# Opening of a fused mLSTM and MoE kernel: v of the first two tiles ahead of q and k on SyncE's queue

## The chip, the cores and the metric

The kernel runs on one core of a Trainium2 chip, in one launch. A core has TensorE (PE), VectorE (DVE), ScalarE (ACT), GpSimd (POOL) and SyncE (SP). PE multiplies matrices, and PEld is its weight load, which overlaps the multiplication. SP and ACT each have a queue of DMA transfers; their issues are listed as SPq and ACTq. A DMA is issued by an instruction of about half a microsecond on its engine and lands some microseconds later. The metric is device time in microseconds (us), as a median of runs; smaller is better.

## What is computed

An mLSTM attention with gates over 2 batches of 8 heads, 768 positions and head size 40, whose output of 1536 x 320 goes through a mixture of four experts and then through a gated MLP:

```python
m_new = np.maximum(f_gate[:, :, t] + m, i_gate[:, :, t])
f_stab = np.exp(f_gate[:, :, t] + m - m_new)
i_stab = np.exp(i_gate[:, :, t] - m_new)
C = f_stab * C + i_stab * np.einsum('bhd,bhe->bhde', vt, kt)
n = f_stab * n + i_stab * kt
y[:, :, t] = o * np.einsum('bhde,bhe->bhd', C, qt) / np.maximum(abs(n . qt), 1.0)
...
out += p[:, e:e + 1] * (np.maximum(x @ w1[e], 0.0) @ w2[e])     # 4 experts, 320 -> 1024 -> 320
...
return (((x @ w_a) * (x @ w_b)) @ w_out)                       # 320 -> 1536 -> 320
```

## The kernel before

**Tiles.** The attention goes by twelve tiles n = 0 to 11, each 128 positions of one batch with its eight heads; tiles 0 and 1 are the first 128 positions of batch 0 and of batch 1. Heads 0 to 3 and 4 to 7 of a tile are its halves hh = 0 and hh = 1. Within a tile the recurrence is worked out as a masked 128 x 128 product of q and k, weighted by exponentials of the gates, times v.

**Loads of a tile.** `load_qk(n, hh)` (L329, its DMA at L341) brings q and k of one half, transposed: of the first four tiles 48 rows of 4096 B, to partitions 0 to 47 for hh = 0 and to partitions 64 to 111 for hh = 1 of one tile `qk_t`. `load_kvo(n)` (L369) reserves the tile `kvo_t` and loads k, v and the carried q in rows; for tiles 0 and 1 it only reserves. Their v comes by `load_v(n)` (L673, DMA at L674): 128 rows of 1476 B. Their k in rows comes much later by `load_k`. `load_gates(j)` (L378) loads gates of position block j into `gt` (DMA at L382 for block 0, on ACT's queue, and L384 for later ones, on SP's). `load_rsel` loads a small selection matrix. The generators `w0`, `w1`, `w2` load the first expert blocks' weights in eight pieces each (L93) and split each piece into a high part `wh` (L78) and a low part `wl` (L102).

**The order.** The first part is not scheduled by a planner. A list `ev` holds (key, function, arguments), is sorted by key, and its functions are called in that order; keys below 0 come before the first expert product. Each function appends its instructions to the engines it uses, and each engine runs its own in that order. So the list's order is the order of each queue. A DMA also takes one of eight semaphores (DMAHW0 to DMAHW7) in turn, and the ninth issue on waits until the earlier DMA with the same semaphore has landed.

**Work of the opening.** In PE's order: eight warm-up products (`warm_up`, L648), four mask products (`mask_of`, L485), the products of q and k of tile 0 (`scores2(0)`, L518, which take the halves by turns), the gate products of tile 0 (`weights_of`, L495), `scores2(1)`, `weights_of` of tile 1, and then the products with v of both tiles (`s2a`, L541), `scores2(2)`, the transposition into x (`s3a`, L154 to L156), and the first expert products (`Item.a`, L210). Beside it DVE works out the gates (`gate1`, L393, on), builds the right operand of `weights_of` (`build_R`, L479, and L477 on ACT), multiplies scores and weights (`s1b`, L530), scales and gates the result (`s2x`, L570 to L580) and writes the low part of x (`split_lo`, L145 and L147). ACT takes the exponentials (`w_exp`, L500). After x of tiles 0 and 1 stands, DVE's next instruction is `gate1(1)`, which needs gates of block 1, and after it comes the eviction `hl` of the first expert product (L278), for whose PSUM buffer the third expert product waits.

Of the kernel before, what the change touches and what calls it, by code (L numbers as in the profile page):

```python
# [13 lines left out]
AF = mybir.ActivationFunctionType  # L14
# [37 lines left out]
def mlstm_moe_kernel(ctx, tc, gates, qk, qc, kvo, dp, w1b, w2b, ident_d, bdmask_d, rsel_d, exp_d, out):  # L52
    nc = tc.nc
# [26 lines left out]
    def piece1(i, s, pool, lo_eng, apart=False, dma=None, hi_eng=nc.scalar):  # L80


        if s == 0:
            wblk[i] = (pool.tile([P, WB1], F32R, tag="wh", name=f"wh{i}"), pool.tile([P, WB1], F32R, tag="wl", name=f"wl{i}"))
        wh, wl = wblk[i]
        st = WB1 // NP1
        cs = slice(s * st, (s + 1) * st)
        at = LAND[i][s] if i < 3 else None
        if at is not None:
            raw = sums[:, at * st:(at + 1) * st]  # L90
        else:
            raw = rawp.tile([P, st], F32, tag="raw", name=f"raw{i}_{s}")
        (dma or nc.sync).dma_start(raw, w1b[i][:, cs])  # L93
        yield
        if apart:
            yield
        copy_on(hi_eng, wh[:, cs], raw)
        yield
        parts = 2 if i < 3 and lo_eng is nc.gpsimd else 1
        for k in range(parts):  # L100
            ps = slice(s * st + k * st // parts, s * st + (k + 1) * st // parts)
            lo_eng.tensor_tensor(wl[:, ps], raw[:, k * st // parts:(k + 1) * st // parts], wh[:, ps].bitcast(F32), op=ALU.subtract)  # L102
# [206 lines left out]
    with ExitStack() as c1:  # L309
# [353 lines left out]
        w0, w1, w2 = ([piece1(i, f, wp0, nc.vector if LOENG[i][f] == "v" else nc.gpsimd, hi_eng=nc.gpsimd if i == 0 and f < 2 else nc.scalar) for f in range(NP1)] for i in range(3))  # L663
# [41 lines left out]
        def x_lo(n):  # L705
# [3 lines left out]
        P_ = nc.gpsimd  # L709
        A_ = nc.scalar  # L710
        ev = [
            (-40, load_gates, 0, A_), (-39.9, load_rsel, nc.sync), (-39.8, load_qk, 0, 0, A_), (-39.7, load_qk, 0, 1, nc.sync),
            (-39.6, load_qk, 1, 0, A_), (-39.5, load_qk, 1, 1, nc.sync), (-39.4, load_kvo, 1), (-39.3, load_kvo, 0), (-39.2, table, AF.Exp),
            (-39.1, load_v, 0), (-39, load_v, 1), (-38.9, go, w0[0:1]), (-38.8, fill_R, 0), (-38.7, ones, ), (-38.6, go, w0[3:4]),
            (-38.5, warm_up, WARM, pw), (-38.4, go, w0[1:2]), (-38.3, go, w0[2:3]), (-38.2, fill_R, 1), (-38.1, load_qk, 2, 1),
            (-38, load_o, 0, nc.sync), (-37.9, load_qk, 2, 0), (-37.8, go, w0[4:5]), (-37.7, go, w0[5:6]), (-37.6, go, w0[6:7]),
            (-37.5, load_ident, ), (-37.4, load_o, 1, nc.sync), (-37.3, go, w0[7:8]), (-37.2, go, w1[0:1]), (-37.1, load_gates, 1),
# [359 lines left out]
```

## Time and profile before

| | |
|---|---|
| median of 3 runs | 598.3 us (597.3, 598.3, 599.43) |
| the profiled execution | 597.87 us |
| its span in the trace | 596.1 us |
| PE busy | 586.3 us (98%) |
| DVE, ACT, POOL busy | 395.2, 268.2, 190.5 us |
| granted clock of PE | 1.0 in all stretches of the page |

The page gives for each engine the time in which it had an instruction running. A busy PE is not PE at its peak. The chain of waits is followed back from the last instruction to what released each step, the timeline lists instructions in order, and a table by stretches gives busy time, the granted clock and what the DMA engines moved. The idle time ahead of an instruction and what ended it stand in brackets.

### The profile page before, as it was taken

What the parts mean: (1) busy time and instruction counts of PE and PEld (TensorE: products, weight loads), DVE (VectorE), ACT (ScalarE), POOL (GpSimd) and SP (SyncE); (2) the same over time, 40 slices, a digit from 0 to 9 for tenths busy, and PEclk for the clock granted to TensorE, in tenths of its full rate; (3) what the DMA queues carried; (4) which work ended last, traced back from release to release, by engine and by line L of the source; (5) the groups of instructions that cost most, each with busy time, mean ns of one, the idle gap of its engine ahead of it and who ended that gap; (6) DMA issues with size and microseconds to landing.
All of it is one profiled execution on the core that took longest, in us unless ns stands there. A gap on an engine that the chain in (4) does not pass through costs nothing.

```text
span 596.1 us, 14965 instructions
## 1 busy us (share of the span) xinstructions
PE 586.3 (98%) x6108; PEld 555.6 (93%) x6108; DVE 395.2 (66%) x813; ACT 268.2 (45%) x606; POOL 190.5 (32%) x246
## 2 busy tenths in 40 slices
PE   8999999999999999999999999999999999999997
PEld 5798999999899999999999999999898989898887
DVE  6888877876423665645466666688688787875444
ACT  7879478683232444433233332334455534341211
POOL 3966665650010333544022231221323222311000
PEclk9999999999999999999999999999999999999999
DMA  8979648750211333332111211515312121200012
GB/s 238 272 227 241 177 135 231 186 154 1 60 40 54 80 86 107 92 89 52 36 40 38 57 40 39 143 53 153 115 42 73 39 58 52 63 21 2 1 38 97
DMA packets 34626, 55.48 MB, mean 93 GB/s; under 512 B 3861, under 2 KB 22461, under 8 KB 34557
## 3 DMA queue, kind: packets, MB, share of 16 engines
q10 hardware_dynamic: 18992, 27.07, 16.4%
q1 hardware_dynamic: 14893, 25.48, 15.9%
q0 software_dynamic: 672, 1.97, 1.2%
q8 instruction: 48, 0.79, 0.6%
q14 instruction: 21, 0.17, 0.1%
HBM read 50.15 MB, written 3.96 MB: 91 GB/s over the span
## 4 chain that ended last, share of the span: by engine, by line
PE 81%; DVE 7%; DMA 6%; ACT 2%; ACTq 2%; issue 2%; SPq 0%; DVEq 0%
PE psa L230 28%; PE psy L255 26%; PE psb L230 8%; PE psa L210 6%; DMA gt<-in_gates 3%; PE pt_y L541 2%; PE psy L289 2%; PE psy L291 2%; PE psy L290 2%; DMA qk_t<-in_qk 2%; PE pt_i L547 1%; PE pt_c L526 1%; PE pt_u L604 1%; DVE acc L300 1%; DVE g L914 1%
## 5 line engine op out<-in xcount | busy, mean ns | idle before, releaser
L255 PE MATMUL psy<-wh,hh 64*128 64x320 f32 x848 | 179.0, 306 | 1.5 <-ACT acc L890 1.5
L255 PE MATMUL psy<-wl,hh 64*128 64x320 f32 x848 | 178.7, 306 | 0.0
L255 PE MATMUL psy<-wh,hl 64*128 64x320 f32 x848 | 178.7, 306 | 0.0
L230 PE MATMUL psa<-xh,wh 64*128 64x512 f32 x648 | 147.5, 388 | 0.2 <-DVE g L914 0.2
L255 PEld LDWEIGHTS psy<-wh,hh 64*128 64x128 f32 x848 | 131.5, 184 | 2.6 <-ACT acc L890 1.9
L255 PEld LDWEIGHTS psy<-wh,hl 64*128 64x128 f32 x848 | 131.6, 184 | 0.0
L255 PEld LDWEIGHTS psy<-wl,hh 64*128 64x128 f32 x848 | 131.4, 184 | 0.0
L230 PE MATMUL psa<-xh,wl 64*128 64x512 f32 x468 | 109.4, 387 | 0.0
L230 PEld LDWEIGHTS psa<-xh,wh 64*128 64x128 f32 x648 | 92.9, 184 | 3.9 <-DVE g L914 0.8
L230 PE MATMUL psa<-xl,wh 64*128 64x512 f32 x432 | 95.3, 387 | 0.0
L911 DVE SCALAR_TENSOR_TENSOR hl<-psa,hh 128x512 fp32r<-128x512 f32 x72 | 46.3, 685 | 72.4 <-ACT hh L910 72.4
L134 POOL TENSOR_TENSOR wl<-tp,lf 128x272 fp32r<-128x272 f32 x48 | 39.1, 814 | 122.3 <-DVE tp L133 111.4
L230 PEld LDWEIGHTS psa<-xh,wl 64*128 64x128 f32 x468 | 69.6, 184 | 2.7
L230 PE MATMUL psb<-xh,wh 64*128 64x512 f32 x216 | 69.7, 388 | 0.0
L131 POOL TENSOR_TENSOR lf<-lf,sq 128x272 f32<-128x272 f32 x48 | 38.1, 795 | 95.4 <-ACT wh L130 72.2
L910 ACT ACTIVATE hh<-psa 128x512 fp32r<-128x512 f32 x72 | 39.1, 596 | 64.1 <-PE psy L255 33.4
L230 PEld LDWEIGHTS psa<-xl,wh 64*128 64x128 f32 x432 | 62.9, 184 | 2.5
L230 PE MATMUL psb<-xh,wl 64*128 64x512 f32 x180 | 58.2, 387 | 0.0
L130 ACT CAST wh<-tp 128x272 fp32r<-128x272 f32 x48 | 20.2, 420 | 68.7 <-DVE tp L127 66.4
L102 POOL TENSOR_TENSOR wl<-raw,wh 128x352 fp32r<-128x352 f32 (+1 forms) x30 | 28.4, 950 | 70.0 <-ACT wh L78 70.0
L230 PE MATMUL psb<-xl,wh 64*128 64x512 f32 x144 | 44.2, 387 | 0.0
L914 DVE TENSOR_TENSOR g<-psa,bs 128x512 f32<-128x512 f32 x36 | 24.7, 685 | 28.1 <-ACT bs L913 27.9
(147 smaller groups left out, 1254.5 us busy)
## 6 DMA issues: line engine op xcount, KB each, us to landing
raw<-in_w2b ACTq DMA_DIRECT2D x48, 272.0 KB, 2.8
qk_t<-in_qk SPq DMA_DIRECT2D x16, 480.0 KB, 6.2
raw<-in_w1b ACTq DMA_DIRECT2D x40, 176.0 KB, 2.3
acc<-in_w1b SPq DMA_DIRECT2D x22, 176.0 KB, 4.8
kvo_t<-in_kvo SPq DMA_DIRECT2D x10, 364.5 KB, 6.2
og_t<-in_kvo SPq DMA_DIRECT2D x6, 320.0 KB, 4.9
dz_t<-z_t ACTq DMA_DIRECT2D x12, 160.0 KB, 2.7
qc_t<-in_qc SPq DMA_DIRECT2D x10, 180.0 KB, 4.3
```

Of the source, the lines that this page charges most:

```text
L102: lo_eng.tensor_tensor(wl[:, ps], raw[:, k * st // parts:(k + 1) * st // parts], wh[:, ps].bitcast(F32), op=ALU.subtract)
L130: nc.scalar.copy(wh[:, cs], tf)
L131: nc.gpsimd.tensor_tensor(lf, lf, sq, op=ALU.mult)
L134: nc.gpsimd.tensor_tensor(wl[:, cs], tf, lf, op=ALU.add)
L210: nc.tensor.matmul(ps, l, r, start=(i == 0), stop=(i == len(prs) - 1))
L230: return nc.tensor.matmul(ps[g], w[rows, o:o + P], x, start=start, stop=stop)
L255: ms = [nc.tensor.matmul(ps[t], l[rows, t * P:(t + 1) * P], w[rows, off:off + DM], start=start, stop=stop) for t, rows in zip(two, (UP, DN))]
L289: nc.tensor.matmul(ps, lh, wh[:, off:off + DM], start=(fi == 0), stop=False)
L290: nc.tensor.matmul(ps, lh, wl[:, off:off + DM], start=False, stop=False)
L910: nc.scalar.activation(hh, ps[f], AF.Relu)
L911: nc.vector.scalar_tensor_tensor(hl, ps[f], 0.0, hh.bitcast(F32), op0=ALU.max, op1=ALU.subtract)
L914: nc.vector.tensor_tensor(g, ps[2 * f + 1], bs, op=ALU.mult)
```

## The change

Nine entries of the list get other keys. `load_kvo(1)`, `load_kvo(0)`, `load_v(0)` and `load_v(1)` come directly behind `load_rsel`, ahead of the four `load_qk` of tiles 0 and 1; the table load for the exponential follows them and keeps its place among ACT's work. No function is changed and no instruction added or removed.

```diff
-            (-40, load_gates, 0, A_), (-39.9, load_rsel, nc.sync), (-39.8, load_qk, 0, 0, A_), (-39.7, load_qk, 0, 1, nc.sync),
-            (-39.6, load_qk, 1, 0, A_), (-39.5, load_qk, 1, 1, nc.sync), (-39.4, load_kvo, 1), (-39.3, load_kvo, 0), (-39.2, table, AF.Exp),
-            (-39.1, load_v, 0), (-39, load_v, 1), (-38.9, go, w0[0:1]), (-38.8, fill_R, 0), (-38.7, ones, ), (-38.6, go, w0[3:4]),
+            (-40, load_gates, 0, A_), (-39.9, load_rsel, nc.sync), (-39.8, load_kvo, 1), (-39.7, load_kvo, 0), (-39.6, load_v, 0),
+            (-39.5, load_v, 1), (-39.4, load_qk, 0, 0, A_), (-39.3, load_qk, 0, 1, nc.sync), (-39.2, load_qk, 1, 0, A_),
+            (-39.1, load_qk, 1, 1, nc.sync), (-39, table, AF.Exp), (-38.9, go, w0[0:1]), (-38.8, fill_R, 0), (-38.7, ones, ), (-38.6, go, w0[3:4]),
```

On SP, at the start of the program: `kvo_t` is v of tiles 0 and 1, `qk_t` the halves hh = 1 of q and k of tiles 0 and 1, and `acc` the first pieces of expert weights, which land in a buffer that later holds sums.

```order
 L680 DMA rsel<-in_rsel_d 112x17
+L674 DMA kvo_t<-in_kvo 128x369 x2
 L341 DMA qk_t<-in_qk 48x1024 x2
-L674 DMA kvo_t<-in_kvo 128x369 x2
 L93 DMA acc<-in_w1b 128x352 [waits DMAHW0_49]
 L93 DMA acc<-in_w1b 128x352 [waits DMAHW1_49]
```

The two loads of v passed the two loads of q and k on SP's queue. ACT's queue, with gates, half 0 of tile 0 and half 0 of tile 1, has the order it had.

On PE, from the last mask products to the first products with v: `pt_c` are scores, `pt_a` the gate products, `pt_y` the products with v.

```order
 L485 MATMUL pt_a<-upper,one 128x512 x3
 L518 MATMUL pt_c<-qk_t 128x128 [waits DMAHW2_49]
-L518 MATMUL pt_c<-qk_t 128x128 [waits DMAHW3_49]
+L518 MATMUL pt_c<-qk_t 128x128 [waits DMAHW6_49]
 L518 MATMUL pt_c<-qk_t 128x128 x6
 L495 MATMUL pt_a<-Rr_110,LT_108 128x512 [waits DVE_49,Activation_49]
 L495 MATMUL pt_a<-Rr_110,LT_108 128x512 [waits Activation_49]
 L518 MATMUL pt_c<-qk_t 128x128 [waits DMAHW4_49]
-L518 MATMUL pt_c<-qk_t 128x128 [waits DMAHW5_49]
+L518 MATMUL pt_c<-qk_t 128x128 [waits DMAHW7_49]
 L518 MATMUL pt_c<-qk_t 128x128 x6
 L495 MATMUL pt_a<-Rr_111,LT_108 128x512 [waits DVE_49] x2
```

PE's order stays. Half 1 of q and k of tile 0 moved from semaphore 3 to 6, that of tile 1 from 5 to 7, and v of the two tiles from 6 and 7 to 3 and 5.

## Rows read from the trace of the kernel before

**Rows 1.** The page's first part: busy time, share of the span, instructions.

```profile
PE 586.3 (98%) x6108; PEld 555.6 (93%) x6108; DVE 395.2 (66%) x813; ACT 268.2 (45%) x606; POOL 190.5 (32%) x246
```

**Rows 2.** The chain of waits, opening: start us, us, what.

```profile
2.21 5.23 DMA qk_t<-in_qk
...
13.53 5.27 DMA gt<-in_gates
...
18.83 0.81 DVE fa L393
...
20.15 0.42 DVE hl L278
```

**Rows 3.** Timeline of PE: start us, us, instruction, count [idle before].

```profile
4.42 2.01 PE L485 MATMUL pt_a<-upper,one 128*128 128x512 f32 x4
6.36 1.16 PE L518 MATMUL pt_c<-qk_t 40*128 40x128 f32 x16
8.00 0.69 PE L495 MATMUL pt_a<-Rr,LT 112*128 112x512 f32 x2 [0.48 <-DVE Rr L479]
8.62 1.16 PE L518 MATMUL pt_c<-qk_t 40*128 40x128 f32 x16
9.72 0.73 PE L495 MATMUL pt_a<-Rr,LT 112*128 112x512 f32 x2
10.38 2.64 PE L541 MATMUL pt_y<-kvo_t,w_t 128*64 128x82 f32 x64
...
20.63 0.39 PE L210 MATMUL psa<-xh,wh 128*128 128x256 f32 x1 [1.05 <-DVE hl L278]
...
24.70 0.39 PE L210 MATMUL psa<-xh,wh 128*128 128x256 f32 x1
```

**Rows 4.** Timelines of ACTq and SPq: issues of the opening.

```profile
1.57 1.08 ACTq L341 DMA_DIRECT2D qk_t<-in_qk  x2
...
1.26 1.00 SPq L341 DMA_DIRECT2D qk_t<-in_qk  x2
2.30 0.90 SPq L674 DMA_DIRECT2D kvo_t<-in_kvo  x2
```

**Rows 5.** Issues of ACTq, single: bytes, us from issue to landing.

```profile
gt<-in_gates ACTq DMA_DIRECT2D x1, 112.0 KB, 3.4
...
qk_t<-in_qk ACTq DMA_DIRECT2D x1, 192.0 KB, 4.6
```

**Rows 6.** Issues of SPq, single, same columns.

```profile
qk_t<-in_qk SPq DMA_DIRECT2D x1, 192.0 KB, 3.8
rsel<-in_rsel_d SPq DMA_DIRECT2D x1, 7.4 KB, 1.7
...
kvo_t<-in_kvo SPq DMA_DIRECT2D x1, 184.5 KB, 5.6
```

**Rows 7.** Busy time by stretches; last columns: granted clock, DMA share, GB/s.

```profile
2.00:7.00 5.00, 5.00 (x21) 2.73 (x21) 2.43 (x8) 3.69 (x5) 0.34 (x2) 1.00 0.91 216
7.00:8.00 1.00, 0.52 (x10) 0.36 (x7) 0.97 (x3) 1.00 (x4) 0.00 (x0) 1.00 1.03 336
8.00:9.00 1.00, 1.00 (x8) 0.68 (x10) 1.00 (x2) 0.56 (x2) 0.00 (x1) 1.00 1.07 393
10.00:11.00 1.00, 1.00 (x18) 0.64 (x19) 0.54 (x2) 0.74 (x2) 1.00 (x3) 1.00 0.99 180
12.00:13.00 1.00, 1.00 (x28) 0.85 (x24) 0.90 (x5) 0.99 (x3) 0.23 (x1) 1.00 0.98 166
```

**Rows 8.** Timeline of DVE and POOL around the first expert products.

```profile
17.73 0.29 DVE L147 TENSOR_TENSOR xh<-pt_x,xh 64x128 fp32r<-64x128 f32 x1
18.83 0.80 DVE L393 TENSOR_TENSOR_SCAN fa<-gt,fa 112x128 f32<-112x128 f32 x1 [0.80 <-DMA gt<-in_gates]
...
15.98 0.24 POOL L78 COPY x_t<-x_t 128x64 f32<-128x64 f32 x1 [0.48 <-DVE x_t L580]
16.17 7.86 POOL L102 TENSOR_TENSOR wl<-acc,wh 128x176 fp32r<-128x176 f32 x14
```

## The prediction

> **What bounds the kernel.** I read the page's first part, then the chain of waits, then the timelines of the first 25 us, then the table by stretches. PE is busy for 586.3 of 596.1 us [rows 1]: a gain or loss must come from the few places where PE stands idle, and the change touches only the opening. In the chain [rows 2] the reader is to see that the opening is a row of transfers, q and k of tile 1 (landed at 7.44), then the gates of block 1 (issued at 13.53, landed at 18.80), then DVE's `fa` and `hl`, which let PE go on. PE's timeline [rows 3] says where PE stood: 0.48 us before the gate products at 8.00, waiting for DVE, and 1.05 us before the third expert product at 20.63, waiting for `hl`. From 20.63 to 25 us it works nearly without gaps, so what the opening adds there is carried on.
>
> **What moves.** Nothing is added or removed. Two loads of v (184.5 KB each) pass two of q and k (192 KB each) on SP's queue [rows 6]. Half 1 of tile 0 was first there, issued at 1.26 [rows 4] and landed after 3.8 us, at 5.1 [rows 6]. Half 0 comes on ACT's queue, issued at 1.57 [rows 4], landed after 4.6 us, at 6.2 [rows 5], and the scores began at 6.36 [rows 3], so half 0 came last and half 1 had 1.3 us to spare. The loads of v landed at about 8.35 (second issue near 2.75, plus 5.6) [rows 4, 6] and were first wanted at 10.38 [rows 3]: v had two microseconds to spare and gains nothing by landing earlier. So the change takes time from the load with 1.3 us of cover and gives it to one with 2.
>
> **When half 1 of tile 0 lands now.** Ahead of its end stand the selection matrix (7.4 KB), the gates (112), two loads of v (369) and itself (192), and, since ACT's queue runs beside SP's and the sizes are alike, also both halves on ACT's queue (384): 1064 KB or 1.09 MB [rows 5, 6]. From 2 to 7 us the queues moved 216 GB/s [rows 7], 1.08 MB by 7.0; the rest is there at 7.03. Landing comes after that. In the old order all of the eight first loads are 1256 KB or 1.287 MB, which at 216 and then 336 GB/s [rows 7] are through at 7.6, and the last landed at 8.35: 0.75 us later. So half 1 lands at 7.8. Low end: the second load on ACT's queue is not ahead of it, 0.89 MB, through at 6.15, landed at 6.9. High end: it takes the place in time of the last load before, 8.35. I take 7.8, for the two queues shared the engines evenly before too: the third load on ACT's queue landed at 7.44 [rows 2], after both of SP's.
>
> **What that moves on PE.** The scores of tile 0 take 1.16 us [rows 3]: 7.8 to 8.96. The gate products behind them on PE stood at 8.00 because of DVE, not because of the scores, which were over at 7.52; that 0.48 us is used up first. They start at 9.0, 1.0 us later (0.1 at the low end, 1.5 at the high). Queued behind the waiting scores on PE are the gate products, the scores of tile 1 and the products with v, and ACT's exponentials and DVE's multiplications wait for these, so all attention work of tiles 0 and 1 goes 1.0 us later. The scores of tile 1 need half 1 of tile 1, the next load on SP's queue: at 173 GB/s (mean of 180 and 166, the two stretches with one such load in flight [rows 7]) it lands 1.14 us after 7.8, at 8.95, and PE comes to these scores 0.62 us after 9.0: 0.65 us of cover.
>
> **What hides it later.** DVE had written x at 18.02 and stood 0.80 us until the gates of block 1 landed [rows 8]. Delayed by 1.0 it is done at 19.02; of the delay 0.8 falls into that idle time. What then counts is when those gates land. The same bytes are ahead of them, but in other company. Before, q and k of both halves went at the same time on two queues, inside the stretch at 216 GB/s; now v runs beside half 0, and the two loads of half 1 come last, mostly alone of their kind, which ran at 173. Two loads are 393 kB: 2.27 us at 173 instead of 1.82 at 216, 0.45 us later. Bounds: all four loads at 173, 0.9 later; or the mixing of v with half 0 gains up to 0.8 (more than 0.80 cannot count, as DVE's idle time is no longer). I take 0.45, since both rates are this kernel's own. The gates land at 19.25, `fa` begins at 19.28, which is behind 19.02, `hl` goes with it, and the third expert product goes from 20.63 to 21.1.
>
> A rule that speaks against the change: the Trainium skill, "SBUF — State Buffer", section "Door 1: The DMA port swizzle", says that partitions 0 to 63 reach only eight of the sixteen ports by which DMA writes and partitions 64 to 127 the other eight. Loads of half 0 and half 1 side by side would then use all ports, and half 1 alone half of them. The trace agrees in kind: 180 and 166 GB/s with one load of 48 rows in flight against 393 with loads of 128 rows [rows 7]. By the page's 27.2 GB/s a port, eight ports give 218 GB/s (an estimate), the two loads would take 1.80 us, the 0.45 would go, and the time would be that of the first rival.
>
> **Other work.** POOL began its long run of low parts behind its copy of x at 15.98 and ended fourteen pieces at 24.03 [rows 8]; the fifth expert product, which takes the last of them, began at 24.70 [rows 3]. Begun 1.0 us later it ends at 25.0, against a product that itself goes to 25.15: 0.15 us of cover are left. The load of weights behind these loads lands some tenths later; POOL and ACT wait for x or for the exponentials there. The gates of block 0 are first on ACT's queue as before; were they earlier, the scores would still be waited for.
>
> **Sum.** Profiled execution 597.87 (span 596.1): +0.45, 598.3. The median of the runs is 0.43 above the profiled one, so 598.3 becomes 598.75; I say 598.8.
>
> **Rivals.**
> - *Hidden.* Half 1 lands by 6.84 (8.00 less the scores' 1.16), PE's 0.48 us covers it, and the gates of block 1 land as before. For it: the low end, 6.9. Against it: the even sharing. Time 598.3.
> - *Faster.* Small rows of v beside half 0 move better than q beside q; the gates of block 1 land up to 0.8 us earlier, DVE's idle time before `fa` goes and the third expert product comes earlier. For it: 393 GB/s with 128-row loads alone [rows 7]. Against it: x must be done early too. 597.5.
> - *Nothing is absorbed.* Half 1 lands at 8.35, the attention is 1.5 us later, and POOL's run of low parts, not DVE, sets the expert products. It decides from about 1.15 us on, where POOL's cover (0.67 us plus the 0.45 of DVE) ends. 0.85 to 1.5 us: up to 599.8.
> - *Slower, by the clock.* PE stands idle from 6.43 (end of the masks [rows 3]) to 7.8 where it had none. The clock reads 1.00, which is 2.4 GHz, in all stretches [rows 7]; if it falls to 1.2 GHz, the gate products, the scores of tile 1 and the products with v (0.69, 1.16, 0.73 and 2.64 [rows 3], 5.2 us) double, and less the 0.8 to 1.0 us that DVE's idle time takes, some 4 us stay: 602.7. It decides from the idle time at which the clock falls. For it: the mask products ran at 0.50 us each, the gate products of the same 512 columns at 0.35, so PE was slower shortly before. Against it: after 1.05 us of idle before 20.63 the clock read nothing else.
>
> **Chances.** Forecast 0.46 (598.5 to 599.1), hidden 0.22, faster 0.08, nothing absorbed 0.15, clock 0.09. The range leaves out the clock and a tail: the faster case less 0.2 is 597.3, nothing absorbed plus 0.5 is 600.3. A measurement of this kernel can tell some 0.3%, 1.8 us, from no change: all cases but the clock lie inside, save the end of the unabsorbed one, so slower 0.15, faster 0.03, same 0.82.
>
> **What would show it.** In the trace after: half 1 of tile 0 landing near 7.8, and PE's scores at L518 waiting for it from 6.43 (right), or starting by 6.84 (hidden); the first gate product at 9.0; v landed long before its first use; DVE's idle time before the second `fa` near 0.25 and gates of block 1 landing near 19.25; third expert product at 21.1. Wrong it is if the third expert product starts before 20.5 or after 22, if the granted clock drops, or if PE's gaps after 25 us change.

## The result, and the profile after

The changed kernel takes 602.82 us (median of 602.55, 602.74, 602.89 and 603.7) beside 598.05 for the kernel before (four runs too); the ratio is 1.008, 95% interval 1.0058 to 1.0101. It is slower by 4.8 us where 0.5 was forecast. The number is that of the rival that was given 0.09, and the clock did fall; that its price came out to 0.1 us is in part luck, as told below.

The profiled execution took 602.74 us, its span 600.9. The timeline of PE answers to [rows 3]; columns as there.

```profile
4.42 1.54 PE L485 MATMUL pt_a<-upper,one 128*128 128x512 f32 x4
5.89 0.49 PE L518 MATMUL pt_c<-qk_t 40*128 40x128 f32 x2
8.75 2.07 PE L518 MATMUL pt_c<-qk_t 40*128 40x128 f32 x14 [2.38 <-DMA qk_t<-in_qk]
10.75 1.22 PE L495 MATMUL pt_a<-Rr,LT 112*128 112x512 f32 x2
11.90 2.08 PE L518 MATMUL pt_c<-qk_t 40*128 40x128 f32 x16
13.91 1.22 PE L495 MATMUL pt_a<-Rr,LT 112*128 112x512 f32 x2
15.06 4.18 PE L541 MATMUL pt_y<-kvo_t,w_t 128*64 128x82 f32 x64
...
24.71 0.39 PE L210 MATMUL psa<-xh,wh 128*128 128x256 f32 x1
```

PE began the scores of tile 0 at 5.89, with half 0 landed, and stood idle for 2.38 us at the first product that needs half 1. What comes then is not only later but slower: the gate products take 1.22 us instead of 0.69, the scores of tile 1 2.08 instead of 1.16, the products with v 4.18 instead of 2.64. The third expert product starts at 24.71, 4.08 us later.

By stretches (last columns granted clock, DMA share, GB/s), which answers to [rows 7]:

```profile
2.00:7.00 5.00, 4.37 (x13) 2.05 (x11) 2.68 (x9) 3.97 (x6) 0.34 (x2) 1.00 0.94 220
7.00:8.00 1.00, 0.00 (x0) 0.00 (x0) 1.00 (x2) 0.79 (x3) 0.00 (x0) 1.00 1.06 159
8.00:9.00 1.00, 0.25 (x2) 0.25 (x4) 0.79 (x2) 0.00 (x0) 0.00 (x0) 0.69 0.98 150
9.00:15.00 6.00, 6.00 (x34) 4.31 (x34) 1.29 (x2) 1.34 (x3) 3.05 (x6) 0.50 1.06 286
15.00:18.00 3.00, 3.00 (x45) 2.94 (x46) 1.65 (x5) 2.97 (x6) 0.00 (x0) 0.50 1.10 359
18.00:19.00 1.00, 1.00 (x24) 1.00 (x22) 0.86 (x3) 1.00 (x3) 0.19 (x1) 0.69 1.09 323
19.00:25.00 6.00, 5.90 (x51) 4.48 (x49) 5.06 (x16) 4.16 (x13) 5.14 (x10) 1.00 0.92 278
```

The granted clock is 1.00, which is 2.4 GHz, until within the microsecond from 8 to 9 us, then 0.50, which is 1.2 GHz, and 1.00 again from within 18 to 19 us: some ten microseconds at the low level, begun while PE stood idle. PE is 100% busy from 9 to 18 us, and this is the stretch in which it loses most. In the kernel before no stretch of the opening shows less than 1.00. For the first microseconds of a run this column does not tell the level, though: the second experiment shows why, and how the products' own times tell it.

The loads, issues and then single issues with the time to landing, answer to [rows 4] and [rows 6]:

```profile
1.27 1.01 SPq L674 DMA_DIRECT2D kvo_t<-in_kvo  x2
2.32 0.89 SPq L341 DMA_DIRECT2D qk_t<-in_qk  x2
```

```profile
kvo_t<-in_kvo SPq DMA_DIRECT2D x1, 184.5 KB, 3.5
...
qk_t<-in_qk SPq DMA_DIRECT2D x1, 192.0 KB, 6.4
```

Half 1 of tile 0 was issued at 2.32 and landed 6.4 us later, at 8.7; in the kernel before it had landed at 5.1. The first load of v landed at 4.8 instead of 7.9 and waited until 15.06.

DVE and POOL at the first expert products answer to [rows 8]:

```profile
22.84 0.29 DVE L147 TENSOR_TENSOR xh<-pt_x,xh 64x128 fp32r<-64x128 f32 x1
23.16 0.53 DVE L393 TENSOR_TENSOR_SCAN fa<-gt,fa 112x128 f32<-112x128 f32 x1
...
21.09 0.24 POOL L78 COPY x_t<-x_t 128x64 f32<-128x64 f32 x1 [0.86 <-DVE x_t L580]
21.28 8.74 POOL L102 TENSOR_TENSOR wl<-acc,wh 128x176 fp32r<-128x176 f32 x14
```

DVE's idle time before `fa` is gone, all 0.80 us of it, and x is written 5.11 us later than before (23.13 against 18.02). Of that 0.80 falls into the idle time, so `fa` starts 4.33 us later; it then takes 0.53 us instead of 0.80, and that leaves PE's delay of 4.08 at the third expert product. POOL's run begins 5.1 us later and takes 8.74 us instead of 7.86.

### The profile page after: what moved, and what is told of

It is laid out like the page before. It is cut to its first block, busy times and chain, and to the rows that moved or that the text cites. A ratio compares the mean times of both kernels' runs of the same rounds, so it can differ in the third digit from the quotient of the medians.

```text
span 600.9 us, 14964 instructions
## 1 busy us (share of the span) xinstructions
PE 590.6 (98%) x6107; PEld 558.0 (93%) x6108; DVE 396.6 (66%) x813; ACT 267.9 (45%) x606; POOL 190.5 (32%) x246
## 4 chain that ended last, share of the span: by engine, by line
PE 83%; DVE 6%; DMA 3%; ACT 2%; issue 2%; POOL 2%; ACTq 1%; SPq 1%; DVEq 0%
PE psa L230 29%; PE psy L255 27%; PE psb L230 8%; PE psa L210 6%; PE pt_y L541 2%; PE psy L289 2%; DMA qk_t<-in_qk 2%; PE psy L290 2%; PE psy L291 2%; POOL wl L102 2%; PE pt_i L547 1%; PE pt_u L604 1%; PE pt_c L526 1%; DVE acc L300 1%; DVE g L914 1%
## 5 line engine op out<-in xcount | busy, mean ns | idle before, releaser
L255 PE MATMUL psy<-wh,hh 64*128 64x320 f32 x848 | 182.9, 306 | 1.1 <-ACT acc L890 1.1
L255 PE MATMUL psy<-wh,hl 64*128 64x320 f32 x848 | 182.8, 306 | 0.0
L255 PE MATMUL psy<-wl,hh 64*128 64x320 f32 x848 | 182.6, 306 | 0.0
L255 PEld LDWEIGHTS psy<-wh,hh 64*128 64x128 f32 x848 | 135.5, 184 | 2.2 <-ACT acc L890 1.5
L255 PEld LDWEIGHTS psy<-wh,hl 64*128 64x128 f32 x848 | 135.6, 184 | 0.0
L255 PEld LDWEIGHTS psy<-wl,hh 64*128 64x128 f32 x848 | 135.6, 184 | 0.0
L230 PEld LDWEIGHTS psa<-xh,wh 64*128 64x128 f32 x648 | 94.4, 184 | 4.4 <-DVE g L914 1.4
```

Of the source, the lines that this page charges most:

```text
L230: return nc.tensor.matmul(ps[g], w[rows, o:o + P], x, start=start, stop=stop)
L255: ms = [nc.tensor.matmul(ps[t], l[rows, t * P:(t + 1) * P], w[rows, off:off + DM], start=start, stop=stop) for t, rows in zip(two, (UP, DN))]
```

## The experiments

All edits are to the list of the opening or to the number of warm-up products. Each ratio is to the kernel before, with runs of both on one chip.

**More warm-up in the changed kernel.** It keeps PE at work until half 1 lands.

```diff
-WARM = 8
+WARM = 16
```

> The changed kernel with sixteen warm-up products on PE instead of eight, so that PE has work until about 8.2 us; all loads in the order of the change. Theory clock: half 1 of tile 0 still lands near 8.7 us, but PE's idle time before the scores is under 1 us, the granted clock stays at 1.00 through the opening, the gate products come at about 9.9 instead of 10.75, the third expert product near 21.8 instead of 24.71, and the time is about 599.3 us. Rival, the late landing alone costs the time: the clock's level in this short stretch matters little, and the time stays at 602 to 603.

Measured: 599.19 us beside 597.46, ratio 1.0025 [1.001, 1.004]. PE's timeline and one stretch:

```profile
6.83 1.28 PE L485 MATMUL pt_a<-upper,one 128*128 128x512 f32 x4
8.04 0.48 PE L518 MATMUL pt_c<-qk_t 40*128 40x128 f32 x2
8.85 1.16 PE L518 MATMUL pt_c<-qk_t 40*128 40x128 f32 x14 [0.32 <-DMA qk_t<-in_qk]
9.93 0.73 PE L495 MATMUL pt_a<-Rr,LT 112*128 112x512 f32 x2
...
21.45 0.38 PE L210 MATMUL psa<-xh,wh 128*128 128x256 f32 x1
...
28.58 0.39 PE L210 MATMUL psa<-xh,wl 128*128 128x256 f32 x1 [0.27 <-POOL wl L102]
```

```profile
9.00:15.00 6.00, 6.00 (x99) 4.86 (x99) 3.34 (x8) 3.84 (x7) 3.06 (x6) 1.00 1.07 285
```

Half 1 lands as late as in the changed kernel, but PE is idle for 0.32 us, the clock reads 1.00, the gate products are at 9.93 and the third expert product at 21.45. The theory of the clock holds. Of the ratio 1.008 the late landing makes 0.0025, 1.5 us, and the clock the other 0.0055, 3.3 us. The version with exchanged halves, below, bears this out: on the same chip, with the same late landing and a fallen clock, it took 602.51 us, 3.3 more. What sixteen warm-up products cost or give by themselves was not tried in the kernel before, so any such effect is inside the 1.5 us. By the medians the late landing costs more than the 0.8 us at the third product (the interval, 0.6 to 2.4 us, includes 0.8). The trace shows where more can come from: PE waits 0.27 us for POOL's low parts at 28.58 and 0.72 us at the gate products at 31.49 for DVE (L530), which waits for POOL in its turn. The kernel before has neither wait.

**A slow clock alone.** The kernel before, with all loads in their old order, and little warm-up.

```diff
-WARM = 8
+WARM = 2
```

> The kernel before with two warm-up products instead of eight; all loads as before, so half 0 lands at 6.2 and half 1 at 5.1. PE runs out of work near 4.3 us and stands idle until the scores at 6.4. Theory clock: the scores and gate products run at half speed for some microseconds though every load lands as before; the time is 600 to 602 us. Rival, landing alone: the opening is as before, 598.1 us.

Measured: 599.4 us beside 597.46, ratio 1.0027 [1.0009, 1.0046]. PE idle for 2.79 us before the scores; scores, gate products and products with v slow. Behind the timeline stands one stretch of the table:

```profile
6.96 2.08 PE L518 MATMUL pt_c<-qk_t 40*128 40x128 f32 x16 [2.79 <-DMA qk_t<-in_qk]
8.97 1.22 PE L495 MATMUL pt_a<-Rr,LT 112*128 112x512 f32 x2
...
13.28 4.58 PE L541 MATMUL pt_y<-kvo_t,w_t 128*64 128x82 f32 x64
...
23.30 0.39 PE L210 MATMUL psa<-xh,wh 128*128 128x256 f32 x1
```

```profile
9.00:15.00 6.00, 6.00 (x48) 4.47 (x48) 3.06 (x5) 3.10 (x5) 3.04 (x6) 1.00 1.07 284
```

The column of the granted clock reads 1.00 here, but the gate products take 1.22 us, as in the changed kernel at 0.50, where they take 0.73 with sixteen warm-up products at 1.00. The trace has no record of the clock before its first change, and the column counts the time without a record as 1.00; here the first record is a rise at 17.7 us. So the clock did not fall in this version, it had not risen yet. The other openings begin at the low level too. The first eight warm-up products take 3.60 us, and three more in the version with eleven add only 0.67. The mask products take 0.50 us each in the kernel before and 0.32 with sixteen warm-up products. The first rise is recorded at 6.0 us in the kernel before and at 5.0 in the changed one. The mean clock of a run does not show such a start: this run's is 0.999.

The time is a little under the 600 to 602 that I gave, but the rival, 598.1 with no change, is out: a slow clock in this opening costs time though the loads keep the old order. Half 0 landed at 6.9 us in this trace and at 6.2 in that of the kernel before, so these times differ by some tenths from run to run; the profiled run, 600.46 us, is also one of the two longest of ten. By the medians the slow clock costs less here, 1.9 us, than the 3.3 of the changed kernel. A likely reason, not shown by a run of its own, is that the opening's slack, PE's 0.48 us and DVE's 0.80, was still there to take some of it, and the late load has used it in the changed kernel.

**One load of v ahead.** The kernel before with `load_v(0)` alone moved.

```diff
-(-39.3, load_kvo, 0) ... (-39.1, load_v, 0)
+(-39.85, load_kvo, 0) ... (-39.82, load_v, 0)
```

> The kernel before with v of tile 0 alone moved ahead of q and k on SP's queue, v of tile 1 behind them. If each load of v that passes costs its share, half 1 of tile 0 lands midway between 5.0 and 8.7, about 6.8; PE is idle before the scores for about 0.5 us, the granted clock stays at 1.00, and PE's 0.48 us before the gate products covers it: 598 us, no change. Rival, that any load of v ahead breaks the opening: clock at 0.5 for about 10 us, 602 us.

Measured: 597.98 us beside 597.46, ratio 1.0008 [0.9994, 1.0023]: no change, as expected, though the clock did fall later, at 16.5 us (last section). Half 1 was issued at 1.72 and took 4.8 us, landed at 6.5. PE was not idle before the scores:

```profile
4.42 2.11 PE L485 MATMUL pt_a<-upper,one 128*128 128x512 f32 x4
6.46 1.31 PE L518 MATMUL pt_c<-qk_t 40*128 40x128 f32 x16
7.75 0.70 PE L495 MATMUL pt_a<-Rr,LT 112*128 112x512 f32 x2
```

With none, one and two loads of v ahead half 1 lands at 5.1, 6.5 and 8.7: 1.4 us for the first and 2.2 for the second. The first is paid by cover that was there; the second is what makes PE stand idle.

**Halves exchanged between the queues.** The changed kernel, with half 1 of tile 1 on ACT's queue and half 0 on SP's.

```diff
-(-39.2, load_qk, 1, 0, A_), (-39.1, load_qk, 1, 1, nc.sync)
+(-39.2, load_qk, 1, 1, A_), (-39.1, load_qk, 1, 0, nc.sync)
```

> The changed kernel with the halves of q and k of tile 1 exchanged between the queues: SP brings v, v, half 1 of tile 0, half 0 of tile 1; ACT brings gates, half 0 of tile 0, half 1 of tile 1. The same bytes are ahead of half 1 of tile 0 on both queues. Theory bytes ahead: it lands near 8.7 again, PE idles 2.4 us, the clock falls, 602 to 603 us. Rival, that two loads of one half one behind the other move slowly because they write the same partitions: the two that remain behind v are of different halves and move side by side, half 1 of tile 0 lands near 7.6, PE idles about 1.2 us; if the clock then holds, about 598.7 us.

Measured: 602.51 us beside 597.46, ratio 1.0081 [1.0057, 1.0106]; half 1 was there at 9.0, PE idle for 2.08 us, and the queues moved 172 GB/s from 7 to 9 us, where the old halves gave 159 and 150 in the changed kernel and 173 and 171 with sixteen warm-up products. So exchanging the halves made no clear difference. The rule of the Trainium skill that I had weighed ("SBUF — State Buffer", "Door 1: The DMA port swizzle") is neither confirmed nor refuted by that, as no view here shows whether the two loads were in flight at the same time; this case leaves open whether it is the ports, the one queue or something else that holds the queues at 150 to 173 GB/s in these two microseconds.

**Less idle time.** The changed kernel with a middle number of warm-up products.

```diff
-WARM = 8
+WARM = 11
```

> The changed kernel with eleven warm-up products instead of eight. Half 1 of tile 0 lands near 8.7 as before, and PE's idle time before the scores shrinks from 2.4 us to about 1.4, the length that the prediction worked out. If that idle time is short enough for the clock, it stays at 1.00 and the time is that of the version with sixteen, about 599.2 us; then the prediction failed because the load landed too late. If the clock falls all the same, near 602 us; then it failed in taking the clock to be unlikely, whatever the landing.

Measured: 599.4 us beside 598.32, ratio 1.0029 [1.0012, 1.0046]. PE was idle for 1.90 us, not 1.4, since the added products run at the high speed, and in the profiled run the clock held:

```profile
8.89 1.16 PE L518 MATMUL pt_c<-qk_t 40*128 40x128 f32 x14 [1.90 <-DMA qk_t<-in_qk]
9.97 0.73 PE L495 MATMUL pt_a<-Rr,LT 112*128 112x512 f32 x2
```

The ten runs differ: six with a mean clock of 0.999 to 1.000 took 598.2 to 599.6 us, four with 0.990 to 0.997 took 600.3 to 602.3. So some runs of this kernel have a fall and some none, but only the profiled run shows where: that the four fell behind this idle time is likely and not shown. A mean of 0.997 does not place a fall. The kernel before has it in seven of its 23 runs on this chip, at 597.7 to 600.3 us, and the last attempt below has it with its only fall at 431 us. The two runs with 0.990 and 0.993 stood longer at the low level.

**Tile 1 out of the way.** The changed kernel with half 0 of tile 1 moved from ACT's queue to SP's end.

```diff
-(-39.2, load_qk, 1, 0, A_)
+(-39.05, load_qk, 1, 0, nc.sync)
```

> The changed kernel with half 0 of tile 1 taken from ACT's queue to SP's, behind half 1 of tile 1. Ahead of half 1 of tile 0 stand 192 KB less. Theory bytes ahead: it lands about 0.9 us earlier, near 7.8, PE idles about 1.4 us, and half 0 of tile 1 lands near 9.8, so that the scores of tile 1 wait for it; the clock decides the time: with the clock at 1.00 about 599.5 us, with the fall about 602. Rival, the last loads of one queue alone set the pace, not the bytes on the other: half 1 of tile 0 lands at 8.5 or later and the time is 602 to 603.

Measured: 601.32 us beside 598.32, ratio 1.0055 [1.0036, 1.0073]. Half 1 of tile 0 was there at 8.27, 0.5 us earlier for 192 KB less on the other queue, between the two expectations; four traces with the full bytes ahead have it between 8.75 and 9.01. PE was idle for 1.81 us and the clock fell:

```profile
8.27 1.83 PE L518 MATMUL pt_c<-qk_t 40*128 40x128 f32 x14 [1.81 <-DMA qk_t<-in_qk]
10.04 1.22 PE L495 MATMUL pt_a<-Rr,LT 112*128 112x512 f32 x2
```

1.81 us of idle time with a fall and 1.90 without: what sets the point is not the length of the idle time alone. In the run without a fall PE had eleven warm-up products behind it instead of eight.

**Two attempts at a faster kernel.** Both start from the kernel before: gates of block 1 ahead of q and k of tile 2, and four more products in PE's idle time at 13 us.

```diff
-(-37.1, load_gates, 1)
+(-38.15, load_gates, 1)
```

> The kernel before with the gates of block 1 loaded ahead of q and k of tile 2 on SP's queue. The rows of before show DVE idle for 0.80 us before it works on these gates, and PE for 1.05 us behind it. If these set the third expert product, it starts at about 19.9 instead of 20.63 and the time falls by about 0.7 us, to 596.8 us beside 597.5, which is at the edge of what can be measured. Rival: scores of tile 2, og or the weights land later by the 113 KB that pass them, and POOL's run of low parts sets the expert products from 24 us on: no change, 597.5 us.

Measured: 597.71 us beside 598.32, ratio 0.9997 [0.9982, 1.0012]. DVE no longer waits for these gates, but the third expert product starts at 20.64 as before. In this run x was 1.0 us late instead. The gates of block 0 landed 0.5 us later, and DVE waited another 0.5 us longer for `og` (0.87 us instead of 0.40, before L580), whose load was issued at 9.4 instead of 7.8: that is the delay which the rival had named. No gain.

```diff
-(-31.9, scores2, 2)
+(-31.95, warm_up, 4), (-31.9, scores2, 2)
```

> The kernel before with four more warm-up products on PE, between the products with v of tiles 0 and 1 and the scores of tile 2, where PE stood idle for 0.6 us before and for 1.3 us in the version with one load of v ahead, whose clock then read 0.57 from 16 to 20 us. Nothing else is changed. If some runs of the kernel before lose time because the clock falls behind this gap, then here the mean granted clock is at 0.999 or above in nearly all runs and the median is about 0.5 us lower, 597.3 beside 597.9. Rival: the gap costs nothing that can be measured, or the added products delay the scores: same time, 597.9.

Measured: 598.25 us beside 598.3, ratio 0.9996 [0.9985, 1.0006]. The clock read 0.999 or more in ten of twelve runs, in the kernel before in nine of seventeen; the time is the same. No version was found that beats the kernel before.

## Why the prediction was wrong

**Where the loss would come from: right.** PE waits at L518 for half 1 of tile 0, v waits unused, and DVE's idle time before `fa` takes 0.80 us of the delay, as the steps said. None of that idle time is left, where some 0.25 us was forecast.

**When half 1 lands: mis-sized.** The step put it at 7.8 with a high end of 8.35; it was 8.7. The rate up to 7 us was as assumed: 220 GB/s from 2 to 7 us is 1.10 MB, where 1.09 was said to be needed. But half 1 of tile 1, next on SP's queue, was issued at 2.8 us and landed at 9.6, so some of these bytes can be its own, and the views do not say how many. So it stays open whether the missing 0.9 us is bytes that were still to come at 7.0 or a longer way from the last byte to the landing. What the rows show is the rate behind v: 159 and 150 GB/s from 7 to 9 us, where the old order, with loads of 128 rows there, moved 336 and 393 [rows 7]. I had used a slow rate for half 1 of tile 1 and not for half 1 of tile 0. That slow rate, 173, was not a clean one either: in its two stretches `og` (320 KB, issued at 7.82, landed at 12.8) was in flight beside the load of 48 rows.

**The idle time and the clock: the step that failed.** The forecast let PE stand idle for 1.4 us and took the clock to hold, with a chance of 0.09 against it; the evidence was one idle time of 1.05 us after which it held. It was 2.38 us, and the clock fell in the profile and, by its mean of 0.991, in all four runs. The sum put the clock at nothing; the runs put it at 3.3 of the 4.8 us. The column's 1.00 was taken as a sign that PE was fast throughout, and the sign that it was not, mask products at 0.50 us each, was named and given little weight. That 1.4 us would have been safe is not shown: 1.81 us with a fall and 1.90 without were measured. The total of the rival, 602.7 beside 602.8 measured, is right in part by luck. It counts some 4 us for the clock, with the four products doubled to 10.4 us, where they took 8.7 (no group doubled: scores 2.08 for 1.16, gate products 1.22 for 0.69) and the clock cost 3.3; and it counts at most 0.45 us for the late load, which cost 1.5.

**What hides the rest: partly, and by another wait.** The 0.45 us of the sum was the later landing of the gates of block 1, which were to be the last that `fa` waits for. They were not: in the changed kernel they landed at 18.85 (18.80 before), long ahead of x at 23.13. With sixteen warm-up products they landed at 19.64, and `fa` came directly behind x:

```profile
19.58 0.29 DVE L147 TENSOR_TENSOR xh<-pt_x,xh 64x128 fp32r<-64x128 f32 x1
19.91 0.52 DVE L393 TENSOR_TENSOR_SCAN fa<-gt,fa 112x128 f32<-112x128 f32 x1
```

With the clock held (sixteen warm-up products) the delay is 1.5 us, not 0.45. The attention is 1.9 us later at the gate products instead of 1.0. DVE's idle time takes its 0.8, but POOL's low parts run on the same delay, and their run, taken to be as long as before, takes 8.73 us instead of 7.86; why is not known. The 0.15 us of cover that the prediction found there was too small for that, and PE waits at 28.58 and 31.49. The changed kernel has the same two waits. Its delay grows there from 4.08 us at the third expert product to 5.2 (34.75 beside 29.54 in the kernel before), and 4.8 are left at the end of the run:

```profile
31.84 0.39 PE L210 MATMUL psa<-xh,wl 128*128 128x256 f32 x1 [0.26 <-POOL wl L102]
...
34.75 0.47 PE L495 MATMUL pt_a<-Rr,LT 112*128 112x512 f32 x1 [0.69 <-DVE w_t L530]
```

That is the rival in which nothing is absorbed; that POOL sets it is read from the traces and was not tried by itself.

## What to carry to other kernels

Before a load is put ahead of another on a queue, work out the new idle time of TensorE behind the one that is passed, and price it twice: as a delay, and as a stretch at the low clock (3.4 to 10.2 us in the falls of these openings). The first load moved ahead was free here and the second was not: the cover of the one that is passed is the number to look up. Filler products on an engine that waits took back some three microseconds here, though they did not make the changed kernel faster than the one before. And read the level of the clock from the times of like products, not only from its column.

## What the runs showed of the hardware that was not expected

In an idle time of 2.38 us, begun at a granted clock of 1.00, the clock fell at 8.4 us and read 0.50 until 18.6, although PE was 100% busy from 9 us on: the slow stretch is several times as long as the idle time. In the version with one load of v ahead the clock read 0.57 from 16 to 20 us after an idle time of 1.31 us at 12.8, and the time did not change. The third expert product, before which the kernel before stands idle for 1.05 us, started only 0.3 us later (20.94). In the version with the gates of block 1 early PE stood idle for 1.43 us at 13.5, and the clock read 1.00 from 14 to 26 us: here too the length of the idle time alone does not decide.

```profile
16.00:20.00 4.00, 3.75 (x16) 3.03 (x17) 2.46 (x7) 2.21 (x6) 3.74 (x8) 0.57 0.90 267
```
